# The low-rank product of an attention-and-mixer kernel, moved onto the two halves of the TensorE array and next to a score chunk

## The chip, the cores and the metric

The kernel runs on one core of a Trainium2 chip. TensorE (PE in the profile, PEld for its weight loads) multiplies matrices into PSUM, which has eight banks. VectorE (DVE), ScalarE (ACT) and GpSimd (POOL) work element by element. SyncE (SP) issues most of the DMAs. Each engine takes its instructions in order, and semaphores tie the engines together. The metric is the device time of one execution in microseconds (us).

## The reference

Sliding-window attention with a few global keys, and on its output a low-rank token mixer with a two-layer channel network:

```python
def _attn_ref(q, k, v, n_global, n_local):          # B=4, H=8, S=768, D=64
    scores = scale * np.matmul(q, k.transpose(0, 1, 3, 2))
    ...                                             # keep 8 global keys and the last 96
    a = np.exp(scores - max); a = a / (sum(a) + 1e-09)
    return np.matmul(a, v)

def _moe_ref(x, U, V, w_ch1, w_ch2):                # x: 4 x 768 x 512, rank 32
    xt = x.transpose(0, 2, 1)
    h = xt @ U @ V                                  # mixes the 768 positions
    u = x + h.transpose(0, 2, 1)
    ch = np.maximum(u @ w_ch1, 0.0) @ w_ch2         # 512 -> 2048 -> 512
    return u + ch
```

The change concerns `h`, more exactly its second factor: the product of the 32-row `xt @ U` with V, and its addition to x.

## The kernel before

The 32 heads are worked in 16 pairs, pair i of batch i // 4. A pair's two heads fill the 128 partitions (64 each), so its score matmuls run over 64 rows each, one head on the upper half of the array and one on the lower, into two PSUM banks.

Pairs 0 to 3 have a loop of their own. From pair 4 on there is one loop, whose step i works on pair i and finishes pair i - 1. The order is written out by hand, and each engine runs its instructions in that order. In one step stand, with units of the channel network between them (`fill`):

- `st_S(i, c)`: three chunks of scores (c = 0, 1, 2), `scores` on TensorE (lines 360 and 367), each followed by two reads on VectorE (line 392) that bring scores and distances to `sp`;
- `st_V(i - 1, hi)`: the weighted sum over v for the previous pair, two heads, into the output bank (`ps_ob`), scaled by VectorE (lines 425, 439) and cast by GpSimd (line 440);
- `st_M1(i - 1)`: `xt @ U` (line 449), cast to `turn16` by VectorE (line 453);
- `st_E(i, hi)`: two exponentials on ScalarE (line 404);
- `st_MT(i - 1)`: the 32-row result turned by TensorE (line 466) and cast to `tmps` (line 467);
- `st_M3(i - 1, g)`: the product with V, line 503, in two halves g of three matmuls. Each writes 384 columns of a bank, and VectorE adds them to x (line 508). After the second GpSimd casts x to 16 bits (line 512);
- `st_X(i - 1)`: a DMA on SyncE that transposes this x into `uT` (line 492), from which the channel network reads;
- `turn(i + 1)`, `load_v`, `load_qk`, `cast_qk`, `st_K`, `st_A`: the transposes by DMA of the next q and k (lines 323, 326), loads of later pairs, their casts on GpSimd (line 122), the copy `kA` on VectorE (lines 335, 336) and the copies `vA` by DMA (lines 302, 303).

A unit of the channel network is either an up-projection (eight matmuls, line 609, then a relu on ScalarE, line 614), or a part of a down-projection (lines 639 and 659, with additions on VectorE, lines 644 and 664). A batch's units are queued once all its four pairs have gone through `st_X`, in step 9 for batch 1, 13 for batch 2 and 17 for batch 3.

PSUM's eight banks are pools: two for scores (`ps_sc`), one for outputs (`ps_ob`), two for down-projections (`ps_cps`) and a ring of three (`ps_th`) for up-projections, and for transposes by TensorE in the steps that have them (`st_T`, line 250, up to step 6). A bank is given again when its last reader is done.

Before that, `load_uv` (lines 209 to 211) loads U and V by two DMAs from GpSimd's queue in the first step. `v16w` holds V in its first 32 rows, zeros in the others.

Of the kernel before, what the change touches and what calls it, by code (L numbers as in the profile page):

```python
# [16 lines left out]
ALU = mybir.AluOpType  # L17
# [3 lines left out]
def kernel(  # L21
# [13 lines left out]
    nc = tc.nc  # L35
    B, H, S, D = q.shape
    NG = int(n_global)
    NL = int(n_local)
    P = 128
# [5 lines left out]
    R = moe_U.shape[1]  # L45
    NP = H // 2
    NPE = 2 * NP
# [14 lines left out]
    GT = S // 2  # L62
    NTG = GT // P
# [16 lines left out]
    def ps_sc(tag="sc"):  # L80
        return psum.tile([P, 512], FP32, name="sc", tag=tag, bufs=2)

    def ps_ob():
        return psum.tile([P, 512], FP32, name="ob", tag="ob", bufs=1)
# [4 lines left out]
    def ps_th(name, dtype=FP32, cols=512):  # L89
        return psum.tile([P, cols], dtype, name=name, tag="th", bufs=3)  # L90
# [35 lines left out]
    def load_v(i):  # L126
        b, h0 = i // NP, 2 * (i % NP)
        st = stp.tile([P, 2 * NSB, D], FP32, name="vst", tag="vst", bufs=2)
        nc.sync.dma_start(
            st, v[b, h0:h0 + 2].rearrange("h (n p) d -> p (h n) d", p=P)  # L130
        )
        vsts[i] = st
# [9 lines left out]
    NPAIR = B * NP  # L142
# [54 lines left out]
    v16w = cst.tile([P, S], FP16, name="v16w")  # L197
# [11 lines left out]
    def load_uv():  # L209
        nc.gpsimd.dma_start(u16[:, :, 0:R], moe_U.rearrange("(c p) r -> p c r", p=P))  # L210
        nc.gpsimd.dma_start(v16w[0:R], moe_V)

    w1_16 = wbig.tile([P, NDC, DFF], FP16, name="w1_16")
    w2_16 = wbig.tile([P, NJC, DM], FP16, name="w2_16")
# [3 lines left out]
    turn16 = [zw[:, i * P:(i + 1) * P] for i in range(2)]  # L218
# [9 lines left out]
    xs, x16s, tmps, uTs = {}, {}, {}, {}  # L228

    def new_batch(b):  # L230
        xs[b] = xp.tile([P, NSB, DM], FP32, name="x_sb", tag="x_sb", bufs=3)
        x16s[b] = xp.tile([P, NP, NSB, P], FP16, name="x16", tag="x16")
        tmps[b] = xp.tile([P, DM], FP16, name="tmp16", tag="tmp16", bufs=3)
        uTs[b] = xp.tile([P, NDC, S], FP16, name="uT", tag="uT")
# [108 lines left out]
    def scores(i, c, on_pe):  # L343

        kT, kA, qT = kts[i], kas[i], qts[i]
        c0 = 512 * c
        tot = min(512, W - c0)
        r0 = 256 if c else 0
        scs = [ps_sc("cps" if on_pe and (i + c) % 2 else "sc") for hi in range(2)]
        if on_pe:  # L350
            for hi in range(2):
                nc.tensor.matmul(
                    scs[hi][:, 0:tot], slI[:, 2 * (i % NP) + hi],
                    rel16.rearrange("p a c -> p (a c)")[:, r0:r0 + tot], start=True, stop=False,
                )
        for kb in (2 * c, 2 * c + 1):
            o = 256 * kb - c0
            for hi in range(2):
                r = slice(hi * D, (hi + 1) * D)
                nc.tensor.matmul(  # L360
                    scs[hi][:, o:o + P], kT[r, kb * P:(kb + 1) * P], qT[r, kb * P:(kb + 1) * P],
                    start=(o == 0 and not on_pe), stop=(o + P == tot),
                )
            if kb < NSB - 1:
                for hi in range(2):
                    r = slice(hi * D, (hi + 1) * D)
                    nc.tensor.matmul(  # L367
                        scs[hi][:, o + P:o + 2 * P], kA[r, kb], qT[r, (kb + 1) * P:(kb + 2) * P],
                        start=False, stop=(o + 2 * P == tot),
                    )  # L370
        return [(sc, c0, tot, r0) for sc in scs]
# [13 lines left out]
    def s_dve(i, hi, got):  # L385
        sc, c0, tot, r0 = got
        if c0 == 0:
            sps[i, hi] = scp.tile([P, W], FP32, name=f"sp{hi}", tag=f"sp{hi}", bufs=1)
        dst, got = sps[i, hi][:, c0:c0 + tot], sc[:, 0:tot]
        if c0 == 512:  # L390
            dst, got = (t.rearrange("p (a c) -> p a c", a=2) for t in (dst, got))
        nc.vector.scalar_tensor_tensor(  # L392
            out=dst, in0=got,
            scalar=qk_scale / slope[2 * (i % NP) + hi], in1=relfs[c0 // 512],
            op0=ALU.mult, op1=ALU.add,
        )

    def st_S(i, c):
        for hi, got in enumerate(scores(i, c, False)):
            s_dve(i, hi, got)  # L400
# [42 lines left out]
    def st_M1(i):  # L443
        b, dc = i // NP, i % NP
        ch = slice(dc * P, (dc + 1) * P)
        if b:
            tps = ps_ob()
            for n in range(NSB):
                nc.tensor.matmul(
                    tps[:, 0:R], x16s[b][:, dc, n], u16[:, n, 0:R],  # L450
                    start=(n == 0), stop=(n == NSB - 1),
                )
            nc.vector.tensor_copy(turn16[i % 2][:, 0:R], tps[:, 0:R])
            return
        tps = ps_th("tmp_ps")
        for n in range(NSB):
            nc.tensor.matmul(
                tps[:, 0:P], u16[:, n], x16s[b][:, dc, n],
                start=(n == 0), stop=(n == NSB - 1),
            )  # L460
        nc.vector.tensor_copy(tmps[b][:, ch], tps[:, 0:P])
# [28 lines left out]
    def st_X(i):  # L490
        b, dc = i // NP, i % NP
        nc.sync.dma_start_transpose(
            uTs[b][:, dc].rearrange("d (n p) -> d n p", n=NSB),
            x16s[b][:, dc].rearrange("p n d -> p (n d)"),
        )

    def st_M3(i, g):
        b, dc = i // NP, i % NP
        ch = slice(dc * P, (dc + 1) * P)
        ups = ps_ob() if g else ps_sc()  # L500
        for t in range(NTG):
            n = NTG * g + t
            nc.tensor.matmul(  # L503
                ups[:, t * P:(t + 1) * P], v16w[:, n * P:(n + 1) * P], tmps[b][:, ch],
                start=(t == 0), stop=(t == NTG - 1),
            )
        dst = xs[b][:, NTG * g:NTG * (g + 1), ch]
        nc.vector.tensor_tensor(  # L508
            dst, ups[:, 0:GT].rearrange("p (t d) -> p t d", t=NTG), dst, ALU.add
        )  # L510
        if g == 1:
            nc.gpsimd.tensor_copy(x16s[b][:, dc], xs[b][:, :, ch])  # L512

    ups_q, downs_q = deque(), deque()
    begun = {}
# [202 lines left out]
    for i in range(NP):  # L718
# [7 lines left out]
        if i == 0:  # L726
            load_uv()
# [46 lines left out]
    for i in range(NP, NPAIR + 2):  # L774
        b, hp = divmod(i, NP)
        live = i < NPAIR
        units = iter(
            (1, 1, 1, 1, 1, 1, 1, 1, 0) if i + 1 < NPE
            else (1, 1, 1, 2, 1, 1, 1, 1, 1) if i < 2 * NP + 1
            else (2, 1, 1, 2, 1, 1, 1, 1, 1)  # L780
        )
        held[0] = i < NP + 3
        if hp == 0 and live and b + 1 < B:
            new_batch(b + 1)
        if live and i > NP:
            st_S(i, 0)
        if NPE <= i + 1 < NPAIR:
            turn(i + 1)
        if i + 1 < NPAIR:
            load_v(i + 1)  # L790
        if i + 2 < NPE:
            load_qk(i + 2)
        fill(next(units))
        if NP < i <= NPAIR:
            st_V(i - 1, 0)
        if i + 1 < NPE:
            st_T(i + 1)
        if i == NP:
            load_w1(2)
        if live:  # L800
            cast_v(i)
            st_A(i)
            if i == NP:
                load_w1(3)
        fill(next(units))
        if live:
            st_S(i, 1)
        fill(next(units))
        if NP < i <= NPAIR:
            st_V(i - 1, 1)  # L810
        if NPE <= i + 3 < NPAIR:
            load_qk(i + 3)
        if i > NP + 1 and (i - 2) % NP == NP - 1:
            queue_ff((i - 2) // NP)
            ahead[0] = 1
        if i == NPAIR + 1:
            break
        fill(next(units))
        if live:
            st_S(i, 2)  # L820
            if i < NPE:
                st_P(i)
        fill(next(units))
        if i > NP:
            st_M1(i - 1)
        if i == NP + 1:
            load_w2(0)
            load_w2(1)
        if i + 2 < NPE:
            cast_qk(i + 2, nc.gpsimd)  # L830
        if live:
            st_E(i, 0)
        fill(next(units))
        if i > NP:
            st_MT(i - 1)
        if NPE <= i + 1 < NPAIR:
            st_K(i + 1)
        fill(next(units))
        if i > NP:
            st_M3(i - 1, 0)  # L840
        if live:
            st_E(i, 1)
        fill(next(units))
        if i > NP:
            st_M3(i - 1, 1)
            st_X(i - 1)
        if i == NP + 1:
            load_w2(2)
            load_w2(3)
        if NPE <= i + 2 < NPAIR:  # L850
            cast_qk(i + 2, nc.gpsimd)
        fill(next(units))
# [38 lines left out]
```

## Time and profile before

| | |
|---|---|
| three timed runs, us | 236.57, 239.76, 233.96 (median 236.57) |
| profiled execution, us | 232.94 |
| its span, first to last instruction | 231.0 |
| TensorE, share of the span | 97% |
| VectorE, ScalarE, GpSimd | 66%, 48%, 35% |
| mean granted clock of TensorE | 1.000 |
| product with V on TensorE (line 503) | 72 matmuls of 219 ns, 8.0 us busy |
| its additions on VectorE (line 508) | 24 of 556 ns |
| the cast behind them on GpSimd (line 512) | 12 of 856 ns |

The profiled execution is one run; the shares and durations below are its own. A matmul's duration reaches from its start to its modelled end, and matmuls overlap, so the time that one costs is the distance to the next start. A line of the timeline has the start (us from the start of the span), the length, the engine, the line of the kernel, the operation, the tile written and those read, the shape, and how many such instructions were merged. A line of the chain has start, length and what the end of the program waited for at that time.

### The profile page before, as it was taken

How to read it: one execution, taken by the hardware profiler on the slowest of the kernel's cores; microseconds unless marked ns; L12 is line 12 of the kernel's file. 1: busy time of each engine (PE TensorE's matmuls, PEld its weight loads, DVE VectorE, ACT ScalarE, POOL GpSimd, SP SyncE). 2: the span in 40 equal slices, each digit the busy share in tenths (PEclk: the TensorE clock that was granted, in tenths of full speed). 3: DMA queues.
4: the chain of work that ended last, by engine and by line, in shares of the span. 5: the costliest groups of instructions: out<-in, count | busy, mean ns of one | idle time of the engine just before them, and what ended most of it. 6: DMA issues, size and time to landing. Idle time of an engine off the chain costs nothing.

```text
span 231.0 us, 5678 instructions
## 1 busy us (share of the span) xinstructions
PE 223.2 (97%) x2324; PEld 161.8 (70%) x2324; DVE 152.7 (66%) x350; ACT 110.9 (48%) x167; POOL 80.5 (35%) x131
## 2 busy tenths in 40 slices
PE   7989999999999999999999999999999999999994
PEld 2455678788644457766666656866688888888883
DVE  3697797868677667566656675779895524444452
ACT  6776957685621313827363707473633334333320
POOL 6399728577444243433424051504120100000000
PEclk9999999999999999999999999999999999999999
DMA  6997998999999999897786955633131302011112
GB/s 183 321 280 201 280 203 188 261 259 175 213 210 244 209 315 216 220 182 188 157 226 134 258 140 145 148 100 79 32 81 48 79 3 91 1 48 45 45 48 91
DMA packets 86561, 36.66 MB, mean 159 GB/s; under 512 B 74152, under 2 KB 83592, under 8 KB 86536
## 3 DMA queue, kind: packets, MB, share of 16 engines
q1 hardware_dynamic: 81480, 32.01, 55.1%
q0 software_dynamic: 5056, 4.29, 12.3%
q8 instruction: 18, 0.29, 0.5%
q14 instruction: 7, 0.06, 0.1%
HBM read 27.46 MB, written 6.29 MB: 146 GB/s over the span
## 4 chain that ended last, share of the span: by engine, by line
PE 86%; POOL 3%; DMA 3%; ACT 3%; DVE 2%; issue 1%; SPq 1%; POOLq 0%
PE hps L609 35%; PE cps L639 22%; PE cx L659 8%; PE cy L659 5%; PE sc L360 4%; DMA vst<-in_v_dram 3%; PE ob L420 2%; PE ob L416 2%; PE sc L367 2%; ACT htr L614 1%; ACT ep L404 1%; PE tp L250 1%; PE sc L503 1%; PE ob L503 1%; SPq L105 1%
## 5 line engine op out<-in xcount | busy, mean ns | idle before, releaser
L614 ACT ACTIVATE htr<-hps 128x512 f16<-128x512 f32 x96 | 56.6, 598 | 85.0 <-PE hps L609 82.2
L609 PE MATMUL hps<-uT,w 128*128 128x256 f16 x756 | 96.2, 273 | 0.5 <-DVE uT L485 0.3
L609 PEld LDWEIGHTS <-w 128*128 128x128 f16 x756 | 70.5, 98 | 11.3 <-issue 0.4
L639 PE MATMUL cps<-w,htr 128*128 128x512 f16 x224 | 56.9, 379 | 0.0
L392 DVE SCALAR_TENSOR_TENSOR sp<-sc,relcat 128x512 f32<-128x512 f32 (+1 forms) x72 | 43.3, 641 | 15.5 <-PE sc L360 8.9
L404 ACT ACTIVATE ep<-sp 128x1408 f16<-128x1408 f32 x24 | 32.8, 1374 | 16.3 <-DVE sp L392 16.3
L512 POOL CAST x<-x_sb 128x768 f16<-128x768 f32 x12 | 10.3, 856 | 60.5 <-DVE x_sb L508 60.5
L639 PEld LDWEIGHTS <-htr 128*128 128x128 f16 x224 | 19.1, 97 | 16.6
L440 POOL CAST x<-x_sb 128x384 f16<-128x384 f32 x30 | 15.8, 525 | 26.8 <-DVE x_sb L439 26.7
L360 PEld LDWEIGHTS <-kT 64*128 64x128 f16 x192 | 8.2, 93 | 15.1 <-issue 13.5
L540 DVE TENSOR_TENSOR s<-htr 128x512 f16<-128x512 f16 x20 | 9.3, 464 | 12.7 <-ACT htr L614 12.7
L439 DVE TENSOR_TENSOR x_sb<-ob,rcp 128x384 f32<-128x384 f32 x30 | 16.7, 558 | 1.0
L659 PEld LDWEIGHTS <-s 128*128 128x128 f16 x160 | 15.5, 98 | 1.8
L360 PE MATMUL sc<-qT,kT 64*128 64x128 f16 x192 | 16.7, 221 | 0.0
L420 PE MATMUL ob<-v,ep 128*128 128x65 f16 x192 | 16.2, 193 | 0.0
L420 PEld LDWEIGHTS <-ep 128*128 128x128 f16 x192 | 13.8, 98 | 2.7 <-ACT ep L379 0.3
L664 DVE TENSOR_TENSOR x_sb<-cx,x_sb 128x256 f32<-128x256 f32 x20 | 8.5, 423 | 10.1 <-PE cx L659 10.0
L136 POOL CAST v<-vst 128x768 f16<-128x768 f32 x16 | 13.4, 839 | 4.5 <-DMA vst<-in_v_dram 4.5
L367 PE MATMUL sc<-qT,kA 64*128 64x128 f16 x160 | 14.1, 216 | 0.9 <-DVE kA L286 0.9
L379 ACT ACTIVATE ep<-sc 128x512 f16<-128x512 f32 (+1 forms) x24 | 12.0, 559 | 5.1 <-PE sc L367 4.8
L416 PE MATMUL ob<-vA,ep 128*128 128x65 f16 x160 | 14.3, 194 | 0.2 <-DVE vA L312 0.2
L659 PEld LDWEIGHTS <-htr 128*128 128x128 f16 x120 | 11.7, 98 | 1.3
(102 smaller groups left out, 269.4 us busy)
## 6 DMA issues: line engine op xcount, KB each, us to landing
qst<-in_q_dram SPq DMA_DIRECT2D x16, 384.0 KB, 4.2
kst<-in_k_dram SPq DMA_DIRECT2D x16, 384.0 KB, 4.9
vst<-in_v_dram SPq DMA_DIRECT2D x16, 384.0 KB, 3.4
out_dram<-x_sb SPq DMA_DIRECT2D x23, 256.0 KB, 2.3
w<-in_moe_w_ch_dram POOLq DMA_DIRECT2D x8, 512.0 KB, 8.9
vA<-v SPq DMA_DIRECT2D x8, 152.3 KB, 4.3
out_dram<-x_sb SPq DMA_DIRECT2D x2, 128.0 KB, 1.7
uT<-x SPq DMA_TRANSPOSE x12, 2.8
```

What stands on the lines that cost most here:

```text
L360: nc.tensor.matmul(scs[hi][:, o:o + P], kT[r, kb * P:(kb + 1) * P], qT[r, kb * P:(kb + 1) * P], start=(o == 0 and not on_pe), stop=(o + P ...
L367: nc.tensor.matmul(scs[hi][:, o + P:o + 2 * P], kA[r, kb], qT[r, (kb + 1) * P:(kb + 2) * P], start=False, stop=(o + 2 * P == tot),)
L392: nc.vector.scalar_tensor_tensor(out=dst, in0=got, scalar=qk_scale / slope[2 * (i % NP) + hi], in1=relfs[c0 // 512], op0=ALU.mult, op1=ALU ...
L404: nc.scalar.activation(ep, sps.pop((i, hi)), AF.Exp, scale=slope[2 * (i % NP) + hi])
L416: nc.tensor.matmul(ob[:, qi], ep[:, OF[qi - 1]:OF[qi - 1] + P], vA[:, qi - 1, hi], start=True, stop=False,)
L420: nc.tensor.matmul(ob[:, qi], ep[:, DG[qi]:DG[qi] + P], vt[:, qi, hi], start=(qi == 0), stop=True,)
L439: nc.vector.tensor_tensor(xo, ob[:, :, 0:D], rb, ALU.mult)
L440: nc.gpsimd.tensor_copy(x16, xo)
L609: nc.tensor.matmul(hps[:, k * FT:(k + 1) * FT], w1_16[:, dc, jt * P:(jt + 1) * P], uT[:, dc, ts], start=(dc == 0 and k == 0), stop=(dc == ...
L614: nc.scalar.activation(cell["htr"][:, 2 * jp:2 * jp + 2].rearrange("p j t -> p (j t)"), hps, AF.Relu)
L639: nc.tensor.matmul(cps, htr[:, jc, t * P:(t + 1) * P], w2_16[:, jc], start=(b > 0 and jc == 0), stop=(jc == NJC - 1),)
L659: nc.tensor.matmul(ps, cell[a][:, j], tw[w][:, j], start=(first and j == 0), stop=(done is not None and j == HJ - 1), skip_group_check=True,)
```

## The change

The product of pairs 4 to 15 now reads 64 rows of V and of its own turned factor, not 128. V is loaded twice, into rows 0 to 31 and 64 to 95. `st_M1` writes its result twice, so that the turned factor stands in both places too. The two halves g of the product read one half of the rows each and are issued in turn, t by t. Their banks are now the output bank and one of the ring.

For pairs 4 to 6 and 8 to 13 the product no longer stands between the two exponentials of step i + 1, but at the start of step i + 2, directly ahead of the first score chunk. The first half's addition comes ahead of that chunk's two reads on VectorE; the second half's, with the cast and the transpose, comes after them. Pairs 7, 14 and 15 keep their step, with the whole product at the place of the second half.

```diff
     def load_uv():
         nc.gpsimd.dma_start(u16[:, :, 0:R], moe_U.rearrange("(c p) r -> p c r", p=P))
         nc.gpsimd.dma_start(v16w[0:R], moe_V)
+        nc.gpsimd.dma_start(v16w[D:D + R], moe_V)
...
-            nc.vector.tensor_copy(turn16[i % 2][:, 0:R], tps[:, 0:R])
+            nc.vector.tensor_copy(
+                turn16[i % 2].rearrange("p (a c) -> p a c", a=2)[:, :, 0:R],
+                tps[:, 0:R].unsqueeze(1).broadcast_to((P, 2, R)),
+            )
...
-    def st_M3(i, g):
+    def st_M3(i):
         b, dc = i // NP, i % NP
         ch = slice(dc * P, (dc + 1) * P)
-        ups = ps_ob() if g else ps_sc()
+        banks = (ps_ob(), ps_th("ups"))
         for t in range(NTG):
-            n = NTG * g + t
-            nc.tensor.matmul(
-                ups[:, t * P:(t + 1) * P], v16w[:, n * P:(n + 1) * P], tmps[b][:, ch],
-                start=(t == 0), stop=(t == NTG - 1),
-            )
+            for g in range(2):
+                n, r = NTG * g + t, slice(g * D, (g + 1) * D)
+                nc.tensor.matmul(
+                    banks[g][:, t * P:(t + 1) * P],
+                    v16w[r, n * P:(n + 1) * P], tmps[b][r, ch],
+                    start=(t == 0), stop=(t == NTG - 1),
+                )
...
+        def add(g):
+            ...
+            if g == 1:
+                nc.gpsimd.tensor_copy(x16s[b][:, dc], xs[b][:, :, ch])
+                st_X(i)
+        return add
...
+        add = st_M3(i - 2) if i > NP + 1 and live and i - 2 != NPE - 1 else None
+        if add:
+            add(0)
         if live and i > NP:
             st_S(i, 0)
+        if add:
+            add(1)
         if NPE <= i + 1 < NPAIR:
             turn(i + 1)
...
-        if i > NP:
-            st_M3(i - 1, 0)
         if live:
             st_E(i, 1)
         fill(next(units))
-        if i > NP:
-            st_M3(i - 1, 1)
-            st_X(i - 1)
+        if i >= NPAIR - 1 or i == NPE:
+            add = st_M3(i - 1)
+            add(0)
+            add(1)
```

Here NP is 4, NPE is 8, NPAIR is 16, NTG is 3 and D is 64.

More of the change, by code (lines that the diff above doesn't have):

```diff
@@ L495, in st_X @@
         )
-    def st_M3(i, g):
+    def st_M3(i):
         b, dc = i // NP, i % NP
         ch = slice(dc * P, (dc + 1) * P)
-        ups = ps_ob() if g else ps_sc()
+        banks = (ps_ob(), ps_th("ups"))
         for t in range(NTG):
-            n = NTG * g + t
-            nc.tensor.matmul(
-                ups[:, t * P:(t + 1) * P], v16w[:, n * P:(n + 1) * P], tmps[b][:, ch],
-                start=(t == 0), stop=(t == NTG - 1),
-            )
-        dst = xs[b][:, NTG * g:NTG * (g + 1), ch]
-        nc.vector.tensor_tensor(
-            dst, ups[:, 0:GT].rearrange("p (t d) -> p t d", t=NTG), dst, ALU.add
-        )
-        if g == 1:
-            nc.gpsimd.tensor_copy(x16s[b][:, dc], xs[b][:, :, ch])
+            for g in range(2):
[6 more added lines that the diff above has]
+        def add(g):
+            dst = xs[b][:, NTG * g:NTG * (g + 1), ch]
+            nc.vector.tensor_tensor(
+                dst, banks[g][:, 0:GT].rearrange("p (t d) -> p t d", t=NTG), dst, ALU.add
+            )
+            if g == 1:
+                nc.gpsimd.tensor_copy(x16s[b][:, dc], xs[b][:, :, ch])
+                st_X(i)
+        return add
     ups_q, downs_q = deque(), deque()
```

## The prediction

> **What bounds the kernel now.** I read the page first, its busy times and the shares of the chain that ended last:
>
> ```profile
> PE 223.2 (97%) x2324; PEld 161.8 (70%) x2324; DVE 152.7 (66%) x350; ACT 110.9 (48%) x167; POOL 80.5 (35%) x131
> ...
> PE 86%; POOL 3%; DMA 3%; ACT 3%; DVE 2%; issue 1%; SPq 1%; POOLq 0%
> ```
>
> TensorE is busy for 97% of the span and is 86% of the chain, so whatever it saves or waits for is paid one to one, unless a later wait gives it back. Its granted clock is 1.000. Busy time of pipelined matmuls hides the cost of one, so I took the timeline of TensorE and subtracted starts from starts:
>
> ```profile
> 59.99 0.33 PE L503 MATMUL ob<-tmp,v16w 128*128 128x128 f16 x3
> 60.25 0.23 PE L360 MATMUL sc<-qT,kT 64*128 64x128 f16 x2
> 60.32 0.22 PE L367 MATMUL sc<-qT,kA 64*128 64x128 f16 x2
> 60.37 0.22 PE L360 MATMUL sc<-qT,kT 64*128 64x128 f16 x2
> 60.43 0.22 PE L367 MATMUL sc<-qT,kA 64*128 64x128 f16 x2
> 60.58 0.39 PE L633 MATMUL cps<-tmp,v16w 128*128 128x512 f16 x1
> ...
> 70.86 0.33 PE L503 MATMUL ob<-tmp,v16w 128*128 128x128 f16 x3
> 71.03 1.03 PE L639 MATMUL cps<-w,htr 128*128 128x512 f16 x4
> ```
>
> Three full-height matmuls of the product take 0.17 us (70.86 to 71.03), 56 ns each. The same three before a score chunk take 0.26: going over to 64 rows costs 0.09. A pair over 64 rows takes 0.05 to 0.07, no more than one full-height matmul, and the last pair before a full-height matmul takes 0.15, so going back costs 0.09 again.
>
> The Trainium skill ("TensorEngine Tiling (Array Packing)", Key Properties) says that a change of the tiling mode drains the engine, while a change of tile alone does not. The trace agrees: about 0.09 us each way, and none between lines 360 and 367, which are different tiles in one mode. If every join paid both drains, nine would lose 1.7 us and the gain below would be gone.
>
> Starts against these prices leave some 8 us of waiting on TensorE, nearly all before 43 us. After that there are only four waits: 0.21 us at 105.83 (the product waits for its turned factor), 0.39 at 176.46, and 0.07 and 0.16 near 171. So after 43 us any new wait counts, and before it the start-up chain does. Its part of the chain in order of time:
>
> ```profile
> 12.08 1.77 POOL u L210
> 13.85 0.53 POOL v16w L211
> 14.38 0.51 POOL x L440
> ...
> 16.96 0.83 POOL q L122
> 17.79 0.78 POOL k L122
> 18.61 0.51 PE tp L250 x6
> ```
>
> GpSimd works without a break from the U load to the casts of q and k for pair 2, and TensorE's transposes wait for them. The issue of V (0.53) stands in that chain.
>
> **The change, part by part.**
>
> *Nine joined products* (pairs 4 to 6 and 8 to 13). Before: 6 x 56 = 336 ns each. After: three pairs at about 60 ns, 180 ns, in the mode of the chunk behind them, so no drain is added. 156 ns saved x 9 = **-1.40 us**. Bounds: nothing if the halves do not overlap, -1.5 at 56 ns a pair. I take 60, from score pairs of the same shape and kind.
>
> *Three products alone* (pairs 7, 14, 15): 180 + 2 x 93 against 336 ns, 3 x 0.03 = **+0.10**.
>
> *The wait at 105.83* (pair 9's product at the end of step 10). There the cast of the turned factor stood behind a 0.69 us addition on VectorE. The product now comes two units of fill later: **-0.21**. The same cover holds at the other joins.
>
> *The second load of V* goes between the first and the cast of x at 14.38, on the chain above. Same shape, so 0.53 us of GpSimd; the load of U, the dearer row, took 1.82, and zero is the bound if a later wait for an input gives it back (GpSimd waited 1.49 us for q at 26.9 to 28.4). The casts, transposes and copies behind it hang on one another, so I take **+0.53**. Its bytes are nothing beside 36.66 MB.
>
> *The cast in the first step* writes 64 instead of 32 numbers a row. Rows: 184 ns at 32, 291 ns at 128, so some 0.03 us more, x12, on VectorE. The transpose behind it comes a unit later (cast done at 47.45, transpose at 47.90). It costs nothing; without that cover, 0.03 at each.
>
> *The banks.* The product took one score bank and the bank of the outputs; now it takes the latter and one of the three banks of the ring that feeds the up-projections. The next user of the output bank comes a fill later and needs the first addition (0.56), which stands first on VectorE: no cost. The ring is where I expect the gain to go. The bank stays taken until the second addition, behind two score reads (1.28 for both) on VectorE, and the up-projections behind it each find a bank one place younger. Three joins meet this. At pair 8's join, into step 10:
>
> ```profile
> 94.56 1.39 ACT L404 ACTIVATE ep<-sp 128x1408 f16<-128x1408 f32 x1
> 95.82 1.09 ACT L614 ACTIVATE htr<-hps 128x512 f16<-128x512 f32 x2
> 96.10 1.05 PE L609 MATMUL hps<-uT,w 128*128 128x256 f16 x8
> ```
>
> The up-projection at 96.10 uses a bank freed at 94.68. After the change it is ready at 95.94, but takes the bank of the one begun at 93.76, whose relu stands behind the exponential and ends at 96.43: **+0.5**. At pair 4's join (50.13, step 6) the q transposes at 51.68, ready at 51.52, wait for a relu that ends at 51.66, and the k transposes behind them take the product's own bank: addition, two reads, addition from 50.15 end at 52.4, against 52.0: **+0.5** together. At pair 12's join, into step 14:
>
> ```profile
> 144.13 0.69 DVE L644 TENSOR_TENSOR x_sb<-cps,x_sb 128x512 f32<-128x512 f32 x1 [0.31 <-PE cps L639]
> 144.74 1.28 DVE L392 SCALAR_TENSOR_TENSOR sp<-sc,relcat 128x512 f32<-128x512 f32 x2
> 146.45 1.03 PE L609 MATMUL hps<-uT,w 128*128 128x256 f16 x8
> ```
>
> The third up-projection takes the product's bank. VectorE has 0.69 + 0.56 + 1.28 + 0.56 to do from about 144.0, ending at 146.85; TensorE is ready at 146.28: **+0.6**. At the other six the ups alternate with downs, or none run near, and the relus are over 1 us ahead (at step 12 the next needs one that ended at 117.72, and starts at 120.2). Bounds: zero, and 1.1 us a join as in the second rival.
>
> The Trainium skill ("TensorEngine Tiling (Array Packing)", Restrictions and Gotchas) warns that row tiling adds PSUM pressure, since tiles must write different banks. The trace so far shows only that the full-height product already took two banks. By the rule the wait is in the evacuation, which is where the three places are.
>
> *The moved x cast and transpose.* The second addition now ends about 2 us later in the step, and with it the cast on GpSimd (0.83) and the transpose on SyncE. The casts of q and k come ahead of that cast on GpSimd. Behind the transpose on SyncE wait the q and k transposes, the v load and the copies of vA. Cover: k's transpose was issued at 134.78, lands 2.5 us later and is read at 141.40; the second copy of vA is issued at 138.96, and landing some 4.4 later leaves nearly 3 us to its use at 146.14. Tightest is batch 2's last transpose: issued at 133.24, now at about 135.2, landing 2.8 later at 138.0, and the fourth up matmul wants it at 137.96. I count zero; without the cover a microsecond. Pair 15's moves by 0.3 us, and had 0.5.
>
> Sum: -1.40 + 0.10 - 0.21 + 0.53 + 0.5 + 0.5 + 0.6 = **+0.6 us**. The profiled execution took 232.94 (span 231.0 and 1.9 around it), so 233.5. The median of the three runs shown is 236.57, 1.0156 times that: **237.2 us**.
>
> **The rivals.**
>
> *The gain stands.* No ring waits, the V load given back: -1.40 + 0.10 - 0.21 = -1.5, so 231.4, or 235.0 on the median's scale. For it: the waits above are 0.5 us each, read from one execution. Against: the GpSimd chain has no idle time from 12 to 18.6 us. 0.17.
>
> *The ring binds at every join.* A relu (0.60) and an exponential (1.37) against one unit of ups (0.87) make 1.10 us. Nine such: -1.5 + 0.53 + 9.9 = +8.9, 241.9, or 245.6. It passes 2% from 0.63 us a join. For it: pair 8's join. Against: in six of nine the relus are ahead. 0.06.
>
> *The moved transposes come late.* A microsecond at batch 2's first up-projection, and up to one each where a k transpose on SyncE holds up the copy of kA (pair 8's was issued at 66.84 and read at 69.46, almost at once) or a copy of vA is late: 1 to 3 us above the forecast, 234.5 to 236.5, or 238.2 to 240.2. 0.12.
>
> *The halves do not overlap*, so that the change does not do what it says: 1.4 above the forecast, 234.9, or 238.6. Against: pairs of this height start 3 ns apart in the score chunks. 0.05.
>
> **The numbers.** The forecast holds 0.60. 2% is 4.7 us, about what a measurement of this kernel can tell from no change: the three runs reach from 233.96 to 239.76, 1.1% below and 1.35% above the median. No sum of mine reaches 4.7 us of gain; 0.06 is left to the spread. Slower by over 2% is the ring at every join (0.06), with the spread on top of late transposes (0.06). The rest, 0.82, is within 2%. The range: 235.0 for the gain kept and 240.2 for late transposes, the lower end a microsecond down for the spread: 234.0 to 240.2.
>
> **What would show it.** Pairs of the product 60 ns apart and no extra 0.09 before the score chunk; the GpSimd chain half a microsecond later at the casts of q and k; TensorE waits of about half a microsecond near 52, 96 and 146 us, the first and the last ended by VectorE's addition and the middle one by a relu; nothing at 105.8. A TensorE idle by microseconds ahead of a first up-projection, or by over 0.6 us at every join, would make the prediction wrong, and so would a V load that leaves the first TensorE transposes where they were.

## The result and the profile after

The changed kernel takes 236.04 us (median of 22 runs, 234.13 to 239.97), the kernel before 235.86 (22 runs, 232.78 to 239.86). The ratio, which leaves out the executions over 1.5% above the fastest of their own kernel (4 of the changed kernel, 10 of the one before), is 1.0064, with an interval of [1.0035, 1.0093]: slower by 0.6%, some 1.5 us (0.8 to 2.2), and within the 2% called no change. Over all 22 executions of each, the medians differ by only 0.18 us. The profiled execution took 235.01 us, its span is 232.9; before it was 232.94 and 231.0.

The busy times and the shares of the chain, from the page of the changed kernel:

```profile
PE 222.7 (96%) x2323; PEld 159.1 (68%) x2324; DVE 151.8 (65%) x350; ACT 110.5 (47%) x167; POOL 80.4 (35%) x132
...
PE 77%; DMA 6%; DVE 6%; ACT 4%; POOL 4%; issue 2%; SPq 1%; DVEq 0%; POOLq 0%
```

TensorE's share of the chain fell from 86% to 77%, and DMA and VectorE stand in it with 6% each: the engine does less and waits more. That it does less is seen at pair 13's product, in the timeline of the changed kernel (start, duration, engine, line, operation, and in brackets the idle time ahead and what ended it):

```profile
156.75 0.23 PE L509 MATMUL ob<-tmp,v16w 64*128 64x128 f16 x1
156.75 0.23 PE L509 MATMUL ups<-tmp,v16w 64*128 64x128 f16 x1
...
156.93 0.22 PE L361 MATMUL sc<-qT,kT 64*128 64x128 f16 x2
```

Three pairs take 0.18 us (156.75 to 156.93), both halves of a pair start together, and the score chunk follows without a further 0.09. The start-up chain of GpSimd, from the chain of waits of the changed kernel, which now has both V loads in it:

```profile
13.47 0.53 POOL v16w L211
14.00 0.50 POOL v16w L212
14.50 0.51 POOL x L441
...
17.86 0.78 POOL k L122
...
18.68 0.51 PE tp L251 x6
```

To see where the rest went I subtracted start from start on TensorE, from pair 6's transposes in step 4 (about 41.2 us) to its last matmul. What an interval has above the price of its shape in the same trace (56 ns for 128 columns, 109 for 256, 216 for 512, 30 for 65, and 95 more where the height changes) is waiting; what is left is own work. Start-up is the time from GpSimd's first cast of v to pair 2's transposes; from those to step 4 every run took 23.31 to 23.35 us, so a delay in the start-up is passed on whole.

| us | start-up | own work | waits after step 4 |
|---|---|---|---|
| before | 7.39 | 185.27 | 1.24 |
| after | 7.83 | 183.88 | 4.52 |
| difference | +0.44 | -1.39 | +3.28 |

Together this is +2.3; 0.37 of it does not show in the span, since v landed that much earlier in this execution (cast at 10.08 against 10.45). The waits of after, and of before, where over 50 ns above the price:

| start, us | extra, us | ended by | in before |
|---|---|---|---|
| 41.82, 42.31 | 0.24 + 0.16 | relus (transposes of k, up-projection) | 0.24 + 0.16 |
| 51.79, 52.28 | 0.20 + 0.16 | relus (transposes of q, k) | none |
| 90.28 | 1.34 | DMA transpose into uT, batch 1 | none |
| 97.80 | 0.55 | relu, step 10 | none |
| 139.32 | 0.22 | DMA transpose into uT, batch 2 | none |
| 162.30 | 0.80 | VectorE's normalisation, step 15 | none |
| 166.90 | 0.25 | VectorE's cast of zw | none |
| 173.97, 178.38 | 0.16 + 0.42 | TensorE's own down-projection (`cy`), VectorE's cast of zw | 0.07 + 0.16 + 0.39 |
| none | 0 | VectorE's cast of tmp | 0.21 at 105.83 |

The waits from 51.79 to 97.80 in the timeline of the changed kernel, in three stretches:

```profile
51.13 1.09 ACT L625 ACTIVATE htr<-hps 128x512 f16<-128x512 f32 x2
...
51.79 0.49 PE L251 MATMUL tp<-ident,q 128*128 128x128 f16 x6
51.99 0.55 DVE L517 TENSOR_TENSOR x_sb<-ups,x_sb 128x384 f32<-128x384 f32 x1
...
52.28 0.50 PE L251 MATMUL tp<-ident,k 128*128 128x128 f16 x6
...
88.62 0.49 PE L620 MATMUL hps<-uT,w 128*128 128x256 f16 x3
...
90.28 0.93 PE L620 MATMUL hps<-uT,w 128*128 128x256 f16 x7 [1.17 <-DMA uT<-x]
...
95.87 1.39 ACT L405 ACTIVATE ep<-sp 128x1408 f16<-128x1408 f32 x1
...
97.14 1.10 ACT L625 ACTIVATE htr<-hps 128x512 f16<-128x512 f32 x2
...
97.80 1.03 PE L620 MATMUL hps<-uT,w 128*128 128x256 f16 x8 [0.48 <-ACT htr L625]
```

In the first stretch the q transposes start after the first relu of the pair and the k transposes after the second (51.13 + 1.09 = 52.22), while the product's second addition still runs to 52.54. In the second, the up-projection of batch 1 does three matmuls, stops for 1.34 us and goes on when the transpose lands. In the third, that of step 10 waits for a relu behind the exponential.

### The profile page after: what moved, and what is told of

The parts are those of the page before. It is cut to its first block, busy times and chain, and to the rows that moved or that the text cites. A ratio compares the mean times of both kernels' runs of the same rounds, so it can differ in the third digit from the quotient of the medians.

```text
span 232.9 us, 5668 instructions
## 1 busy us (share of the span) xinstructions
PE 222.7 (96%) x2323; PEld 159.1 (68%) x2324; DVE 151.8 (65%) x350; ACT 110.5 (47%) x167; POOL 80.4 (35%) x132
## 4 chain that ended last, share of the span: by engine, by line
PE 77%; DMA 6%; DVE 6%; ACT 4%; POOL 4%; issue 2%; SPq 1%; DVEq 0%; POOLq 0%
PE hps L620 32%; PE cps L650 18%; PE cx L670 8%; PE cy L670 5%; DMA vst<-in_v_dram 3%; PE sc L361 3%; DMA uT<-x 3%; ACT ep L405 2%; PE ob L421 2%; ACT htr L625 2%; PE ob L417 2%; DVE sp L393 1%; PE ob L509 1%; PE sc L368 1%; PE tp L251 1%
## 5 line engine op out<-in xcount | busy, mean ns | idle before, releaser
L650 PEld LDWEIGHTS <-htr 128*128 128x128 f16 x224 | 19.4, 97 | 17.4
L517 DVE TENSOR_TENSOR x_sb<-ob,x_sb 128x384 f32<-128x384 f32 x12 | 6.7, 556 | 13.2 <-PE ob L509 11.9
```

The costliest lines, as they stand in the source:

```text
L650: nc.tensor.matmul(cps, htr[:, jc, t * P:(t + 1) * P], w2_16[:, jc], start=(b > 0 and jc == 0), stop=(jc == NJC - 1),)
```

## The experiments

Every run's ratio is to the kernel before on the same chip; start-up, own work and waits are of its profiled execution, as above.

| run | ratio [95%] | start-up | own work | waits |
|---|---|---|---|---|
| after_again | 1.0115 [1.0049, 1.0181] | 7.79 | 183.88 | 3.83 |
| vload_only | 1.0216 [1.0147, 1.0284] | 7.83 | 185.26 | 5.58 |
| v_late | 1.0113 [1.0050, 1.0177] | 7.32 | 183.90 | 5.63 |
| pair6_own | 1.0065 [1.0015, 1.0115] | 9.04 | 184.10 | 3.17 |
| halves_own | 1.0033 [0.9991, 1.0076] | 7.85 | 185.41 | 3.65 |
| join_full | 1.0026 [0.9976, 1.0076] | 7.34 | 185.28 | 6.65 |
| ring_spared | 1.0041 [0.9995, 1.0087] | 7.89 | 183.93 | 3.92 |
| w2_early | 1.0012 [0.9958, 1.0066] | 7.38 | 185.31 | 7.46 |
| pair13_own | 1.0033 [0.9990, 1.0077] | 8.11 | 184.08 | 4.40 |
| adds_first | 1.0023 [0.9969, 1.0077] | 7.80 | 183.95 | 3.40 |
| five_joined | 0.9888 [0.9803, 0.9973] | 8.10 | 184.43 | 1.71 |
| five_again | 0.9977 [0.9851, 1.0102] | 7.33 | 184.44 | 4.36 |

Most intervals overlap, so the times alone order few of these kernels. Own work repeats to 0.07 us among runs whose matmuls are the same, and single waits can be found again by their place; the readings below rest on those. In pair6_own, pair13_own and five_joined the start-up holds another delay: GpSimd's cast of x waits there for VectorE (0.66, 0.15 and 0.66 us), and a load of V took 1.37 to 1.40 us to issue.

**after_again**: the changed kernel once more.

> The changed kernel once more. Theory A (the ledger of its first profile): against before, nine joins save 1.4 to 1.5 us and the wait at 105.8 goes (-0.2), and new waits of TensorE give it back and more: transposes near 52 us 0.36, the up-projection of step 10 near 98 us 0.55, the first up-projection of batch 1 near 90 us 1.34 and of batch 2 near 139 us 0.22, the weighted sum of pair 14 near 162 us 0.80. If that is how the kernel works, each of these five waits comes back within 0.3 us, and the ratio is 1.004 to 1.009. Rival B: the long waits at 90 and 162 us are of one execution; then they are missing here or elsewhere, and only the ring's two come back.

Every wait came back: 0.21 + 0.15 at 52.31 and 52.80, 0.55 at 97.61, 0.23 at 139.14, 0.80 at 162.12, 0.25 at 166.72, each within 10 ns of the first profile. Only batch 1's differs, 0.64 at 90.10 against 1.34, which is outside the 0.3 that was expected, and the ratio, 1.0115, is above 1.004 to 1.009, though its interval reaches into that. So the waits belong to the program; the size of that one depends on the execution.

**vload_only**: the kernel before with the second load alone.

```diff
         nc.gpsimd.dma_start(v16w[0:R], moe_V)
+        nc.gpsimd.dma_start(v16w[D:D + R], moe_V)
```

> The kernel before, with the second load of V alone. My step: 0.53 us on GpSimd's chain from 12 to 18.6 us, passed on to the end: the first transposes of pair 2 come 0.4 to 0.6 us after those of before when counted from the end of the cast of v at the chain's head, and the span grows by 0.4 to 0.6 (ratio 1.002). Rival: a wait for an input or for exponentials later in the start-up takes it back, and the ratio is 1.000.

The start-up is 7.83, as in the changed kernel (+0.44), and own work is that of before. But the ratio is 1.0216 where 1.002 was expected, more than the whole change. The timeline of vload_only:

```profile
64.41 1.02 PE L640 MATMUL cps<-w,htr 128*128 128x512 f16 x4 [0.93 <-DMA w<-in_moe_w_ch_dram]
...
67.47 1.86 PE L640 MATMUL cps<-w,htr 128*128 128x512 f16 x4 [1.70 <-DMA w<-in_moe_w_ch_dram]
```

TensorE waits 0.99 and 1.86 us for two loads of the second weights, which landed at 64.4 and 67.4 (60.2 and 63.5 in before), and then runs its matmuls 0.43 us apart in place of 0.216; some 1.5 us of the 5.58 in the table are this slower pace. w2_early waits as long for the same weights without a second load of V, so the load is not needed for it. The changed kernel, which has the load, has no such wait in either profile, but it also issues these two loads 2 us sooner (49.71 against 51.83; see w2_early). Why all six runs of vload_only were long (236.81 to 239.75; the kernel before, beside them, had a median of 237.13 and reached 239.63) is open.

**v_late**: the changed kernel, with the second load issued in step 4, off the start-up chain.

```diff
-        nc.gpsimd.dma_start(v16w[D:D + R], moe_V)
...
                 load_w1(3)
+                nc.gpsimd.dma_start(v16w[D:D + R], moe_V)
```

> The changed kernel with the second load of V issued from GpSimd in step 4, behind the last load of the first weights, where GpSimd has gaps. If the load costs 0.5 us where it stands, this is 0.4 to 0.5 us faster than the changed kernel, ratio about 1.004, and the casts of q and k for pair 2 come 0.5 us sooner after the head of the chain. If the start-up takes it back, it is the same as the changed kernel (1.006).

The start-up fell to 7.32, so the load's issue was worth 0.5 there, as forecast. The kernel is not faster: the waits rose to 5.63, with 0.32 for second weights at 65.20, 0.30 for GpSimd's cast of x at 68.69, 0.33 for qT at 73.19 and 1.52 for uT at 91.72. Right on the chain, wrong on the time.

**pair6_own**: pair 6's product is done at its old place, by itself.

```diff
-        add = st_M3(i - 2) if i > NP + 1 and live and i - 2 != NPE - 1 else None
+        add = st_M3(i - 2) if i > NP + 1 and live and i - 2 not in (6, 7) else None
...
-        if i >= NPAIR - 1 or i == NPE:
+        if i >= NPAIR - 1 or i - 1 in (6, 7):
```

> The changed kernel with pair 6 also keeping its own step (whole product at the place of the second half, as pair 7). Theory A: the 1.34 us wait near 90 us comes from SyncE's queue, which pair 6's later transpose (issued at 75.44, 74.08 before) pushes back, so that pair 7's transpose was issued at 87.01, not when its cast was done at 84.7. Then here pair 7's is issued by 85.3 and the wait near 90 us is gone or under 0.2, for 0.16 to 0.2 us of lost joining: span 1.0 to 1.2 less than the changed kernel's. Rival: the wait comes from pair 7 itself, whose two halves now stand together at the later place; then it stays above 1 us.

The wait near 90 is gone and no other changed by over 10 ns. SyncE's queue in the changed kernel:

```profile
72.78 1.82 SPq L633 DMA_DIRECT2D out_dram<-x_sb  x2
...
75.44 1.21 SPq L496 DMA_TRANSPOSE uT<-x  x1
...
79.36 1.68 SPq L129 DMA_DIRECT2D vst<-in_v_dram  x1
...
83.86 0.83 POOL L521 CAST x<-x_sb 128x768 f16<-128x768 f32 x1 [5.68 <-DVE x_sb L517]
...
84.93 1.95 SPq L633 DMA_DIRECT2D out_dram<-x_sb  x1
...
87.01 1.30 SPq L496 DMA_TRANSPOSE uT<-x  x1
```

In the kernel before:

```profile
74.08 1.31 SPq L492 DMA_TRANSPOSE uT<-x  x1
...
78.14 0.58 SPq L129 DMA_DIRECT2D vst<-in_v_dram  x1
...
82.87 1.43 SPq L622 DMA_DIRECT2D out_dram<-x_sb  x1
...
84.42 1.29 SPq L492 DMA_TRANSPOSE uT<-x  x1
```

In pair6_own:

```profile
73.03 2.17 SPq L633 DMA_DIRECT2D out_dram<-x_sb  x2
...
75.29 1.29 SPq L496 DMA_TRANSPOSE uT<-x  x1
...
79.50 0.90 SPq L129 DMA_DIRECT2D vst<-in_v_dram  x1
...
84.29 1.42 SPq L633 DMA_DIRECT2D out_dram<-x_sb  x1
...
85.83 1.30 SPq L496 DMA_TRANSPOSE uT<-x  x1
...
89.11 1.91 PE L620 MATMUL hps<-uT,w 128*128 128x256 f16 x16
```

Against the kernel before, pair 6's transpose is issued 1.36 us later. Behind it on SyncE the v load comes 1.22 later, and with a longer issue of that load (1.68 against 0.58) and of a store (1.95 against 1.43) pair 7's transpose 2.59 later, at 87.01 for 84.42. Its x was cast by 84.69, but the store stood ahead of it. TensorE was ready at 88.95, and it landed at 90.25 (87.01 and 3.24 of transfer, by the chain). In pair6_own it is issued at 85.83, and the up-projection runs through from 89.11. (It was expected by 85.3.)

The run does not show, though, that the move made the wait. Pair 6's x is cast 1.8 us sooner in it (done at 73.61 against 75.41), but its transpose is issued only 0.15 us sooner, since stores keep SyncE busy until 75.20. Most of the 1.18 us at pair 7's transpose comes from the shorter issues of the v load and the store (0.90 and 1.42). In the changed kernel SyncE stands idle from 74.60 until that cast, so there the late cast held the queue by some 0.75 us of the 1.34; in after_again it stands idle only from 75.84 to 75.96, and TensorE waits 0.64 us all the same. Over all profiles the wait is 0.64 to 2.02 us in the seven with pair 6 joined, and 0, 0, 0, 0.11, 0.31, 0.57 (halves_own) and 1.69 (w2_early) in the seven that leave it at its old place. So the join goes with longer waits, but SyncE has little to spare there without it, and what sets the size is open. And the time did not fall: 1.0065 against 1.0064.

**pair13_own**: the same for pair 13, with 13 in place of 6 in the two lists.

> The changed kernel with pair 13 also keeping its own step. Theory A: the waits of step 15 near 162 us (0.80, the weighted sum of pair 14's second head for the output bank) and 167 us (0.25) come from VectorE, which in that step also makes the sums of weights and now gets the two additions on top, where it had made them before the step began. Then both fall below 0.15, for 0.16 to 0.2 of lost joining: 0.7 to 0.9 us less from step 4 to the end, apart from the wait near 90, which moves from run to run. Rival F: the sums of weights alone fill VectorE there (the kernel before waits 0.4 near 176 us for the same reason), and a wait above 0.4 stays.

The waits of 0.80 and 0.25 in step 15 are 0.07 and 0.17. VectorE in the changed kernel:

```profile
157.67 1.28 DVE L393 SCALAR_TENSOR_TENSOR sp<-sc,relcat 128x512 f32<-128x512 f32 x2
...
158.87 0.55 DVE L517 TENSOR_TENSOR x_sb<-ups,x_sb 128x384 f32<-128x384 f32 x1
...
159.33 0.68 DVE L655 TENSOR_TENSOR x_sb<-cps,x_sb 128x512 f32<-128x512 f32 x1
...
159.93 1.61 DVE L551 TENSOR_TENSOR t<-w,t 128x1024 f16<-128x1024 f16 x2
...
161.68 0.56 DVE L440 TENSOR_TENSOR x_sb<-ob,rcp 128x384 f32<-128x384 f32 x1
...
162.30 0.20 PE L421 MATMUL ob<-v,ep 128*128 128x65 f16 x1 [0.63 <-DVE x_sb L440]
```

In pair13_own:

```profile
157.81 0.56 DVE L517 TENSOR_TENSOR x_sb<-ob,x_sb 128x384 f32<-128x384 f32 x1 [0.15 <-PE ups L509]
158.29 0.55 DVE L517 TENSOR_TENSOR x_sb<-ups,x_sb 128x384 f32<-128x384 f32 x1
...
159.35 1.28 DVE L393 SCALAR_TENSOR_TENSOR sp<-sc,relcat 128x512 f32<-128x512 f32 x2
...
161.15 1.28 DVE L551 TENSOR_TENSOR t<-w,t 128x1024 f16<-128x1024 f16 x2
...
162.57 0.56 DVE L440 TENSOR_TENSOR x_sb<-ob,rcp 128x384 f32<-128x384 f32 x1
...
163.28 0.19 PE L421 MATMUL ob<-v,ep 128*128 128x65 f16 x1
```

In step 15 VectorE also forms weighted sums of weights (line 551) for the last feed-forward. The joined product puts its second addition (0.55) behind the score reads, and with it the down addition and the sums move back; the reciprocal (161.47) and the normalisation (161.68) come behind 1.61 us of sums, and TensorE needs the output bank that they empty. With the product at its old place both additions are done before the score reads (157.81 and 158.29 against 159.35), and 0.72 us of the 0.80 go. From step 4 to the end, without batch 1's wait (2.02 here), this is 0.6 us less, where 0.7 to 0.9 was expected.

**join_full**: the products stay joined, with additions, banks and order as changed, but over the full height of 128 rows: one load of V, the old cast, and

```diff
-                n, r = NTG * g + t, slice(g * D, (g + 1) * D)
+                n, r = NTG * g + t, slice(0, P)
```

> The changed kernel with the product over all 128 rows again (and V loaded once), at the new place and into the new banks. Theory A: it has every wait of the changed kernel near 52, 90, 98, 139 and 162 us (within 0.3 each, but for the one near 90, which moves from run to run) and lacks the gain: six matmuls of 56 ns, so 0.15 us more at each of nine joins (+1.35) against 0.45 less for the load of V. TensorE's end 0.5 to 1.3 us after the changed kernel's. Rival D: the halves on both sides of the array do not overlap as score pairs do, and the full-height product is as fast.

Timeline of join_full at pair 13's product:

```profile
160.43 0.22 PE L505 MATMUL ob<-tmp,v16w 128*128 128x128 f16 x1
...
160.71 0.22 PE L505 MATMUL ups<-tmp,v16w 128*128 128x128 f16 x1
...
160.86 0.23 PE L360 MATMUL sc<-qT,kT 64*128 64x128 f16 x2
...
166.08 0.20 PE L420 MATMUL ob<-v,ep 128*128 128x65 f16 x1 [0.47 <-DVE x_sb L439]
```

Six matmuls take 0.43 us to the score chunk, and own work is 185.28, as before (185.27): no gain. The waits are there: 0.19 at 52, 0.38 at 101.06, 0.07 at 142.93 (batch 2's) and 0.64 at 166.08, each some 0.16 less than in the changed kernel, about what the longer product takes; 0.21 at 170.64, and batch 1's with 1.76 at 93.55. So the gain is from the halves, and the waits are from the place and the banks. The time does not show the lost gain: TensorE's end came 3.7 us after the changed kernel's, not 0.5 to 1.3, since this execution also waited for loads and casts (0.90 at 66.01, 0.82 at 70.02), and the ratios, 1.0026 and 1.0064, have overlapping intervals.

**halves_own**: the opposite; all products on halves, at their old places. The loads of the second weights are issued behind the casts of q and k of that step in this run.

```diff
-        add = st_M3(i - 2) if i > NP + 1 and live and i - 2 != NPE - 1 else None
+        add = st_M3(i - 2) if False else None
...
-        if i >= NPAIR - 1 or i == NPE:
+        if i > NP:
```

> The changed kernel with all twelve products in their own step (the halves at once, at the place of the second half), none joined to a score chunk; the last two loads of the second weights are issued behind the casts of q and k, where the changed kernel has them in effect. Theory A: each product costs 180 + 2 x 93 ns against 336, so the joining was the whole gain and is gone (+0.03 x 12 against before), the V load costs 0.45, and the waits of the changed kernel near 52, 90, 98, 139 and 162 us are all absent (under 0.15 each), because the ring's bank is taken at another time and the transposes are about where they were. Span 231.2 to 232.2. Rival C: the waits come from the halves or the ring's bank as such, not from the place; then some of those at 90, 98 and 162 stay.

None of the waits at 52, 98 and 139 is there, and at 162.74 it is 0.07. So these come from the place at which the product is done, and not from the halves or the ring's bank as such. Own work is 185.41, 0.14 above before: 12 products alone cost some 0.01 us each. So the join is what saves the drains. The wait for uT near 90 stays, with 0.57 at 90.92, where none was expected. The other waits are new, 1.43 for second weights at 65.71 and 0.33 at 56.93 for a cast on GpSimd, and the span is 233.3, not 231.2 to 232.2.

**ring_spared**: two joined products take a bank of the down-projections in place of the ring's.

```diff
-        banks = (ps_ob(), ps_th("ups"))
+        banks = (ps_ob(), ps_cps("ups") if i in (4, 8) else ps_th("ups"))
```

> The changed kernel with the second half of pairs 4 and 8 in a bank of the down-projections, not of the ring. Theory A: the up-projection of step 10 (near 98 us, 0.55) and the transposes of step 6 (near 52, 0.36) wait for a ring bank one place younger; with the ring spared, the wait near 98 is gone (under 0.1) and that near 52 falls below 0.1, and the other waits stay: 0.7 to 0.9 us gained. Rival E: ScalarE's exponential itself holds the step (its results are wanted next), and the wait moves to the next instruction that needs it.

The waits near 52 and 98 are gone, so they are the ring's. But a new one of 0.33 stands at 56.51, where the U product of step 6 waits for GpSimd's cast of x (line 441): the 0.36 of step 6 were mostly cover for that cast, and only step 10's 0.55 were gained, not 0.7 to 0.9.

**adds_first**: the product's second addition goes ahead of the score reads.

```diff
         if add:
             add(0)
+            add(1)
         if live and i > NP:
             st_S(i, 0)
-        if add:
-            add(1)
```

> The changed kernel with both additions ahead of the score chunk and its reads, so that the second half's addition, the cast and the transpose come about 1.3 us sooner and the score reads 0.56 later. Theory A: the late transposes come from the place behind the two reads; then the wait near 139 us (0.22) goes and that near 90 falls below 0.5 or goes; the transposes near 52 keep the part that ScalarE causes; the wait near 98 us (0.55, a relu behind an exponential) stays, and that near 162 us stays above 0.5. Rival G: the reads are what must not wait; then chunk 1 of the scores waits for its banks, with new waits of 0.1 to 0.5 us in several steps, and nothing is gained.

The waits at 52 and 139 are gone, that of step 15 fell from 0.80 to 0.47, and that of step 10 stayed (0.54): it ends with a relu and not with an addition. Two things came otherwise than expected. Batch 1's wait stayed, with 0.82 at 89.87. And near 52 nothing was left, though relus had ended the wait there: the two relus run as they did (51.21 to 52.30), and the transposes start at 51.67 and 52.00, ahead of their ends. It seems that with the addition earlier the transposes are given other banks of the ring; the records do not number them. The cast of x costs 0.32 at 57.31, as in ring_spared. The waits total 3.40, against 4.52 and 3.83 in the two profiles of the changed kernel.

**w2_early**: the kernel before, with the loads of the second weights issued behind the casts of q and k.

```diff
+        if i == NP + 1:
+            load_w2(2)
+            load_w2(3)
...
-        if i == NP + 1:
-            load_w2(2)
-            load_w2(3)
```

> The kernel before with nothing of the change but one side effect of it: the last two loads of the second weights are issued from GpSimd behind the casts of q and k, at about 49.7 us, not behind the product's cast at 51.7. If the landing of these loads (63.5 us in the profile of before, first needed at about 64 to 67) is what some executions wait for, it lands about 2 us sooner here and the ratio is 0.985 to 1.000, with fewer executions above 236 us. If not, the ratio is 1.000 and the spread is the same.

No gain: 1.0012 [0.9958, 1.0066]. They were issued only 0.55 us earlier (51.15 against 51.70), since the load of q came late and GpSimd waited 1.53 us for it; the last landed at 67.9. Its profile waits 1.70 and 1.85 for them. So this run did not test an issue 2 us sooner.

Over all profiles, the wait for these weights goes with the issue of their loads. In the seven that issue the first by 50.41 us there is none in six and 0.32 us in v_late; in the seven that issue it at 51.13 or later there is none in one, the kernel before, and 0.38 to 3.55 us in six. The changed kernel is of the first kind (49.71, against 51.70 before), because its cast of pair 4's x now stands behind these loads on GpSimd. So the change may spare a wait that the kernel before has in some executions; no run separates this from the rest.

**five_joined** and **five_again**: the kernel before, with the new product for pairs 5, 8, 9, 10 and 12 only. Pair 8's second half takes a bank of the down-projections, since its join had the wait of step 10; at the other four no wait had been found. The second load of V is issued in step 4.

```diff
+    JOINED = (5, 8, 9, 10, 12)
...
+        add = st_MJ(i - 2) if live and i - 2 in JOINED else None
...
+                nc.gpsimd.dma_start(v16w[D:D + R], moe_V)
...
-        if i > NP:
+        if i > NP and i - 1 not in JOINED:
```

> The kernel before with the joined product for pairs 5, 8, 9, 10 and 12 alone (pair 8's second half in a bank of the down-projections), the other seven as before over 128 rows, and the second load of V in step 4. Theory A: 5 x 0.156 + 0.21 = 1.0 us less of TensorE from step 4 to the end than before (185.7 us of its own work becomes 184.9, and the wait near 106 is gone), with none of the waits near 90, 98, 139 and 162 us and nothing added to the start: ratio 0.995 to 0.997. Rival: each join costs its saving in waits elsewhere, and the ratio is 1.000 or above.

> The kernel with five joined products once more, for its interval. Theory A from TensorE's own work gives 0.995 to 0.997 (1.0 us of 233); 0.989, as first measured, would need 2.5 us, more than the joins and the wait near 106 us can give. Rival: the first figure was the spread of few executions, and it is 1.000.

Own work is 184.43 and 184.44, 0.84 less than before: five joins at 0.17. None of the waits of the change are left but batch 1's, at 0.31 and 0.11. The first ratio, 0.9888 [0.9803, 0.9973], is more than the 1.0 us of the account can give, though its interval reaches down to that; the second is not resolved, 0.9977 [0.9851, 1.0102]. The second profile has a price of the late load, in the timeline of five_again:

```profile
47.83 1.04 PE L641 MATMUL hps<-uT,w 128*128 128x256 f16 x8
...
49.52 0.34 PE L511 MATMUL sc<-tmp,v16w 128*128 128x128 f16 x3 [0.65 <-DMA v16w<-in_moe_V_dram]
```

The product of pair 4 waits 0.82 us for V, and the second weights came late too (0.46 and 1.81 at 64.29 and 67.30). 0.84 us less work on TensorE is shown; that the kernel is faster is not settled.

## Why the prediction was right in sign, and where its sizes were wrong

The forecast was +0.6 us and within 2%; measured +1.5 (0.8 to 2.2). The sum holds two errors that partly cancel: ring waits counted 0.7 too high, and waits counted at nothing that came to 2.6 and 1.9 in the two profiles. That the forecast is no further off is partly luck. The time itself, 236.04 for 237.2, lies below the forecast although the change cost more: the scale of 1.0156 came from three runs whose median, 236.57, lies above the 235.86 of 22.

- *Joined and single products, -1.40 + 0.10*: right. Own work fell by 1.39 in both profiles of the changed kernel, and join_full and halves_own show that it takes both the halves and the join. The rule that a change of mode drains the engine (the Trainium skill, "TensorEngine Tiling (Array Packing)", Key Properties) agrees with this trace: the joined pairs pay no drain of their own, the single ones two, and own work rose by some 0.01 a product where all stood alone. The single ones were counted at 0.03.
- *The wait at 105.83, -0.21*: right; there is none near 106.
- *The second load of V, +0.53*: right, 0.44 in vload_only and 0.5 back in v_late; the start-up alone shows it, the times do not.
- *The ring, +0.5 at pair 8's join*: right in size and in its relu (0.55), and gone in ring_spared.
- *The ring, +0.5 at pair 4's join*: 0.36. The q transposes wait for a relu as forecast. The k transposes do too, not for the product's second addition: they start at 52.28, and it ends at 52.54. And it hides 0.33 of another wait, so it cost little.
- *The ring, +0.6 at pair 12's join*: did not come. The step "the third up-projection takes the product's bank" failed: it started at 147.47 without a wait, while the addition ran from 147.25 to 147.80. Both misses are in the same step, the counting of which bank comes round next; the records do not number the banks.
- *The moved transposes, 0*: the step "I count zero" failed, twice. Batch 2's last transpose, named as the tightest, was by its own figures 0.04 late (138.0 against 137.96) and cost 0.22; it is gone in adds_first. Batch 1's cost 1.34 and 0.64 and was not looked at: I followed SyncE's queue behind the moved transpose to the q and k transposes, the v load and the copies of vA, but not on to the next step's transpose 10 us later, which stands behind the same queue. How much of it is the move's stays open: by the trace some 0.75 of the 1.34, and almost nothing of the 0.64; w2_early (1.69) and halves_own (0.57) have it without the move. The rival of late transposes was thus right for a part, at the low end of its price, and the 1.34 us ahead of a first up-projection's fourth matmul come near to what the prediction named as a sign of being wrong.
- *The output bank and "the other six", 0*: the step that looked at up-projections and relus alone failed. At pair 13's join the load on VectorE decides, with the sums of weights that only the late steps have; it cost 0.80 + 0.25, and pair13_own takes 0.80 of these 1.05 away.

The other rivals fell: by the ratio the gain did not stand, no ring wait passed 0.6, and the halves overlap.

What stays open: the sizes of the waits for loads between 60 and 92 us, which differ from execution to execution by up to 2 us, whether the sooner issue of the second weights helps the changed kernel, and with both whether any of the partly joined kernels beats the one before.

## What to carry to other kernels

A product over half the rows gains only next to other work of the same height; at its own place the drains take it back. When a step is moved, follow each queue it is moved in (here SyncE's and VectorE's) until something has slack again, in every later step and not only in the tightest, and list what else that engine does in the very step, and what now comes sooner (here two weight loads on GpSimd). An experiment that takes a wait away shows its cause only if the rest of the queue ran alike in both executions. A wait that is taken away shows its worth only when it is known what was late behind it.

## What the runs showed of the hardware

In vload_only TensorE's clock fell to half after waits of 0.99 and 1.86 us with 1.2 us of matmuls between. The windows of vload_only (busy time and number of instructions of each engine, granted clock, DMA share, GB/s):

```profile
66.00:67.50 1.50, 0.03 (x1) 0.03 (x1) 0.56 (x2) 0.00 (x0) 0.00 (x0) 0.88 1.24 254
67.50:69.00 1.50, 1.50 (x4) 0.52 (x4) 0.00 (x0) 0.00 (x0) 0.36 (x1) 0.50 1.01 230
69.00:70.70 1.70, 1.70 (x5) 0.59 (x4) 0.69 (x1) 0.00 (x0) 1.64 (x3) 0.54 1.23 274
70.70:72.00 1.30, 1.30 (x12) 0.53 (x11) 0.61 (x2) 0.00 (x0) 0.02 (x1) 1.00 1.16 234
```

If the clock was either whole or half, these means make 0.36 + 1.50 + 1.56 = 3.4 us at half, from about 67.1 on. In five_again (waits of 0.46 and 1.81) and w2_early (1.70 and 1.85) the clock stayed at 1.00 over the same stretch. The Trainium skill ("TensorE: Matmul & The Clock Gate", Part 1) has the clock halved after an idle window of about 3.4 us that runs freely, and back after a busy one. The return agrees. The fall does not: in the 3.4 us before it TensorE had matmuls from 64.41 to 65.8, so here the stretch was not idle throughout. Why one run of the three shows the fall, no run tells.

The same DMA takes SyncE very different times to issue: the v load ahead of pair 7's transpose 0.58, 0.90 and 1.68 us (before, pair6_own, after), the store ahead of that transpose 1.42 to 1.95, and one load of q 6.36 in the kernel before and 7.01 in vload_only. Behind each stands all the rest of the queue in order.
